# Early chunks of a fused retention, attention and spectral kernel in another order: V of chunk 0 behind the visit of chunk 1, the loads of chunk 1 ahead of V's weights, the decay table made by ScalarE, no second warm-up

## The chip, the cores and the metric

The kernel runs on one core of a Trainium2 chip. A core has TensorE (PE, matrix products), VectorE (DVE), ScalarE (ACT), GpSimd (POOL) and SyncE (SP, which issues nearly all transfers), each with its own list of instructions that it works off in order. The metric is the device time of one execution in microseconds (us). TensorE's clock has two levels, 1.2 and 2.4 GHz; the profile gives the level that was granted as 0.50 or 1.00.

## The reference

Three stages follow each other. All is float32, the batch is 8, the sequence 576, the width 512 (8 heads of 64).

```python
# 1: retention (8 heads)
scores = q @ k.T / 8
ret = scores * Dmat              # gamma[h] ** (i - j) for i >= j, else 0
x = ret @ v                      # heads side by side: [8, 576, 512]
# 2: four experts, two of them per token by x @ w_gate
for e in range(4):
    a = softmax(causal(x @ wq[e] @ (x @ wk[e]).T / 8))
    out += weight[..., e] * (a @ (x @ wv[e]) @ wo[e])
# 3: mixing
theta = out @ w_theta
y = w_tok_r @ (out * cos(theta)) + w_tok_i @ (out * sin(theta))
u = out + y
result = u + relu(u @ w_ch)
```

## The kernel before

Retention is computed in chunks of 128 tokens, five per batch (the last has 64), with a running state. For a chunk there are, all on PE with 64x64 tiles: the **scores** of its two halves (`ret_scores`, line 143), two **states** (`ret_state`, line 158, products of the chunk's k with its decayed v, called `vp`), and the **values** (`ret_values`, lines 173 and 180, which use the masked scores `sm`, `vp` and the states). A **visit** of chunk c here means the call of `ret_first` that computes the values of chunk c, interleaved product by product with the second state of c, and with the scores and the first state of chunk c+1. The result is scaled by a decay table `gt` (line 190, DVE) to `xt`, and split into a high and a low part `xh` (ACT, line 192) and `xl` (POOL, line 193), because the later products are run as three products of rounded parts.

`vp` is made by POOL in `scale()` (line 128) from the loaded `kv`. The table `gt` is loaded for 128 tokens and extended to the other chunks by `make_gt` (line 439). For stage 2, `proj_v` (line 273, "V of chunk c": 12 products of 128x260) and `proj_qk` (line 245) multiply `xh` and `xl` with the parts `WH`, `WL` of the expert weights; these parts are made from the loaded `wst` by ACT and DVE (lines 106 and 107), the columns of V first.

Batch 0 has no earlier work to hide behind. Its five chunks are written out by hand at the head of the program: the order of the calls is the order on PE, which is scheduled by hand there. On the other engines and on SP's queue an instruction stands where the call put it, or behind the one named by `issue_after`. Loads are issued by SP in the order written (`loads`, lines 117 and 120, is k and q, then k and v of a chunk); there are buffers for four chunks, so the load of the first chunk of batch 1 waits until the values of chunk 1 are done. `warm_up(n)` runs n small products on zeros.

The stretch that the change touches reads so before:

```python
ret_first(0, -1, (0, 0), [(0, 1)])      # scores and first state of chunk 0
ret_first(0, 0, None, [])               # second state and values of chunk 0
...                                     # split of V's weights, vp of chunk 1
warm_up(WARM2)
work(-1, "v0")                          # V of chunk 0
...
ret_first(0, -1, (0, 1), [(2, 3)])      # scores and first state of chunk 1
...
ret_first(0, 1, (0, 2), [(4, 5)])       # visit of chunk 1
...
ret_first(0, 2, (0, 3), [(6, 7)])       # visit of chunk 2
...
work(-1, "v1")                          # V of chunk 1
ret_first(0, 3, (0, 4), [(8,)])         # visit of chunk 3
work(-1, "v2 k00")
```

After that the batches run as a pipeline: attention of batch b beside the retention of batch b+1.

Of the kernel before, what the change touches and what calls it, by code (L numbers as in the profile page):

```python
# [15 lines left out]
AF = mybir.ActivationFunctionType  # L16
# [4 lines left out]
B, H, S, D = 8, 8, 576, 64  # L21
E, DM = 4, 512
C = 128
# [13 lines left out]
LDB = 4  # L37
# [8 lines left out]
         ("v0", "R3"), ("v1", "O"), ("v2 k00", "R4"), ("q00", "R5"), ("v3 k01 v4 g", "O")]  # L46
PTV = (0,)
WARM = 50
WARM2 = 10
WB = 8  # L50
JOBS = (58, 75)

# [11 lines left out]
def tile_kernel(ctx: ExitStack, tc: tile.TileContext, qk, kv, w1, wo, wot, wd, cst, out):  # L64
    nc = tc.nc
# [23 lines left out]
    gam = att.tile([128, NCH, 2, 4], F32, name="gam")  # L89
# [7 lines left out]
    gt = ret.tile([128, 4, S], F32, name="gt")  # L97
# [12 lines left out]
    MARK = {}  # L110
    QKT, KVT, XT, VP, SM, RAW = {}, {}, {}, {}, {}, []

    def loads(b, c):
        R = ROWS[c]
        o = c * 1024
        t = ret.tile([128, 8 * R], F32, name="kt", bufs=LDB, padded_shape=[128, 1024]).rearrange("p (h r) -> p h r", h=8)
        nc.sync.dma_start(t, qk[b, :, o:o + 8 * R].rearrange("p (h r) -> p h r", h=8))
        n = R // 64
        u = ret.tile([128, 2, 2, 256], F32, name="kv", bufs=LDB)
        nc.sync.dma_start(u[:, :n], kv[b, c, :, :n * 512].rearrange("r (j a d) -> r j a d", j=n, a=2))  # L120
        QKT[b, c], KVT[b, c] = t, u
        RAW.append((b, c))

    def scale():
        b, c = RAW.pop(0)
        n, u = ROWS[c] // 64, KVT[b, c]
        vp = ret.tile([128, 2, 4, D], F32, name="vp", bufs=VPB)
        MARK["pool"] = nc.gpsimd.tensor_mul(vp[:, :n], u[:, :n, 1, :].rearrange("p j (h d) -> p j h d", h=4),
                                            gam[:, c, :n, :, None].to_broadcast([128, n, 4, D]))
        VP[b, c] = vp  # L130

    def half(x):
# [2 lines left out]
    def ret_scores(b, ks):  # L135

        n = len(ks)
        ps = ps1.tile([128, n, 4, 64], F32, name="w", bufs=WB, padded_shape=[128, 2, 4, 64])
        for i, k in enumerate(ks):
            t, j = QKT[b, k // 2], k % 2  # L140
            for x in range(4):
                for s in range(2):
                    nc.tensor.matmul(ps[half(s), i, x, :], t[half(s), 4 + x, half(j)], t[half(s), x, half(j)],  # L143
                                     start=True, stop=True, skip_group_check=True)
                yield
        sm = ret.tile([128, n, 4, 64], F32, name="sm", bufs=4, padded_shape=[128, 2, 4, 64])
        MARK["sm"] = nc.vector.tensor_mul(sm, ps, tri[:, None, None, :].to_broadcast([128, n, 4, 64]))  # L147
        for i, k in enumerate(ks):
            SM[b, k] = sm[:, i]

    def ret_state(b, k):

        c, j = divmod(k, 2)
        u, vp = KVT[b, c], VP[b, c]
        pS = ps1.tile([128, 4, D], F32, name="w", bufs=WB, padded_shape=[128, 4, 128])
        for x in range(4):
            for s in range(2):
                nc.tensor.matmul(pS[half(s), x, :], u[half(s), j, 0, x * D:x * D + D], vp[half(s), j, x, :],  # L158
                                 start=x == 0, stop=x == 3, skip_group_check=True)
            yield  # L160
        o = SB[(k + 1) % 4]
        MARK["S"] = nc.vector.tensor_add(o, pS, SB[k % 4]) if k else nc.scalar.activation(o, pS, AF.Copy)

    def ret_values(b, c):

        R = ROWS[c]
        t, vp = QKT[b, c], VP[b, c]
        px = ps1.tile([128, 4, R], F32, name="w", bufs=WB, padded_shape=[128, 4, 128])
        for j in range(R // 64):
            sm = SM.pop((b, 2 * c + j))  # L170
            for x in range(4):
                for s in range(2):
                    nc.tensor.matmul(px[half(1 - s), x, half(j)], vp[half(s), j, x, :], sm[half(s), x, :],
                                     start=j == 0 and x == 0, stop=False, skip_group_check=True)
                yield
        for j in range(R // 64):
            k = 2 * c + j
            for x in range(4 if k else 0):
                for s in range(2):
                    nc.tensor.matmul(px[half(1 - s), x, half(j)], SB[k % 4][half(s), x, :], t[half(s), x, half(j)],  # L180
                                     start=False, stop=False, skip_group_check=True)
                yield
        for x in (QKT, KVT, VP):
            x.pop((b, c))
        cs = slice(c * C, c * C + R)
        if c == 0:
            XT[b] = (w1p.tile([128, 4, S], F32R, name="xh", bufs=1),
                     w1p.tile([128, 4, S], F32R, name="xl", bufs=1))
        xt = ret.tile([128, 4, R], F32, name="xt", bufs=2, padded_shape=[128, 4, 128])
        MARK["xt"] = nc.vector.tensor_mul(xt, px, gt[:, :, cs])  # L190
        xh, xl = XT[b]
        MARK["xh"] = nc.scalar.activation(xh[:, :, cs], xt, AF.Copy)  # L192
        MARK["xl"] = nc.gpsimd.tensor_sub(xl[:, :, cs], xt, xh[:, :, cs])  # L193
        nx = (b, c + LDB) if c + LDB < NCH else (b + 1, c + LDB - NCH)
        if nx[0] < B:
            loads(*nx)
# [19 lines left out]
    def ret_first(b, c, nx, scores):  # L216

        diag, off = [], []
        if c > 0:
            scale()  # L220
        if 0 <= c < NCH - 1:
            diag.append(ret_state(b, 2 * c + 1))
        diag += [ret_scores(nx[0], ks) for ks in scores]
        if nx and nx[1] < NCH - 1:
            diag.append(ret_state(nx[0], 2 * nx[1]))
        if c >= 0:
            off.append(ret_values(b, c))
        for _ in zip_longest(chain(*diag), chain(*off)):
            pass
# [74 lines left out]
    def work(b, names):  # L304
        for n in names.split():
            x = b + n.islower()
            if x < B:
                if n in "Gg":
                    gate(x)
                elif n[0] == "T":  # L310
                    token_tile(ps1, 0, len(X2))
                elif n[0] == "F":
                    fuse(int(n[1]))
                elif n[0] in "Vv":
                    proj_v(x, int(n[1]))
                else:
                    proj_qk(x, int(n[1]), int(n[0] in "Kk"), int(n[2]))
# [98 lines left out]
    def warm_up(n):  # L416
        pw = ps1.tile([128, 128], F32, name="w", bufs=WB, padded_shape=[128, 512])
        for _ in range(n):
            nc.tensor.matmul(pw, warm, warm, start=True, stop=True)
# [12 lines left out]
    gf = w1s.tile([128, 4, NCH], F32, name="gf")  # L432
# [3 lines left out]

    def make_gt(c):
        R = ROWS[c]
        nc.vector.tensor_mul(gt[:, :, c * C:c * C + R], gt[:, :, :R], gf[:, :, c, None].to_broadcast([128, 4, R]))

    wst = {}

    def load_w1(a, z):
        wst[a] = w1s.tile([128, 4, z - a], F32, name=f"wst{a}", bufs=1)
        nc.sync.dma_start(wst[a], w1.rearrange("(k p) n -> p k n", p=128)[:, :, a:z])

    def split_w1(a, k):
        t = wst[a]
        sl = slice(a, a + t.shape[2])
        split(WH[:, k, sl], WL[:, k, sl], t[:, k])  # L450

    load_w1(512, NW1)
    for c in range(1, LDB):
        loads(0, c)
    load_w1(0, 512)
    nc.sync.dma_start(tie, cst[:, o + 1088:o + 1088 + E * E].rearrange("p (a b) -> p a b", a=E))
# [75 lines left out]
    def fuse(p):  # L532
        acc = ps1.tile([128, DM], F32, name="w", bufs=WB)
        for kt, (th, wt) in enumerate(FW):
            mm3(acc, wt[:, 0, p, :], wt[:, 1, p, :], th[:, 0, :], th[:, 1, :], kt == 0, kt == 3)
        split(MH[:, p, :], ML[:, p, :], acc)

    ret_first(0, -1, (0, 0), [(0, 1)])
    ret_first(0, 0, None, [])
    for k in range(2):  # L540
        with tc.issue_after(MARK["xt"].ins), tc.issue_after(MARK["xh" if k else "S"].ins):
            split_w1(512, slice(2 * k, 2 * k + 2))
    with tc.issue_after(MARK["xl"].ins):
        scale()
    warm_up(WARM2)
    work(-1, "v0")
    with tc.issue_after(MARK["split"].ins):
        make_gt(1)
    ret_first(0, -1, (0, 1), [(2, 3)])
    scale()  # L550
    with tc.issue_after(MARK["pool"].ins):
        nc.gpsimd.dma_start(cm, cst[:, o:o + 1088])
    with tc.issue_after(MARK["sm"].ins):
        make_gt(2)
    ret_first(0, 1, (0, 2), [(4, 5)])
    for c in range(3, NCH):
        with tc.issue_after(MARK["xt"].ins):
            make_gt(c)
    ret_first(0, 2, (0, 3), [(6, 7)])
    for k in range(4):  # L560
# [92 lines left out]
    for t in range(nu + 1):  # L653
        b, k = divmod(t, 10)
        if b < B - 1:
            more, between, after = *SLOTS[k], ""
        else:
            b = B - 1
# [22 lines left out]
        if b < B - 1:  # L681
            if between[:1] == "R":
                c = int(between[1])
                x = b + 1
# [14 lines left out]
        i = int(t >= JOBS[0])  # L699
        x = t - JOBS[0] if i else t - 2  # L700
# [284 lines left out]
```

## Time and profile before

| | us |
|---|---|
| median of 3 runs | 880.44 |
| lowest and highest run | 877.99 and 881.26 |
| the profiled execution's own time | 879.58 |
| its span, first to last instruction | 877.8 |
| PE busy in the span | 859.2 (98%) |
| DVE, ACT, POOL busy | 622.0, 454.6, 218.7 |

The span is what the trace covers; 1.78 us of the execution's time lie around it. A busy share of 98% says that PE is the engine that sets the time, so what matters is where PE stands still or runs at the lower clock. "issue" in the profile is time in which an engine waited for nothing that the profile shows.

### The profile page before, as it was taken

Reading aid. Unit: us, or ns where it says so; the run is one execution under the profiler, and the core shown is the slowest. Engines: PE = TensorE matmul, PEld = TensorE weight load, DVE = VectorE, ACT = ScalarE, POOL = GpSimd, SP = SyncE. Lnnn points to the kernel's source line nnn. Section 1 sums busy time; section 2 is a strip of 40 time slices with the busy share of each in tenths; the row PEclk is TensorE's granted clock in tenths of the full one; section 3 lists DMA queues with packets and bytes.
Section 4 is the critical chain, followed back from the end, with each engine's and each line's share of the span. In section 5 each row is a group of like instructions: output and inputs, shape, how many; then the busy total and the mean of one; then the engine's idle time right before and its main releaser. Section 6 shows DMA issues by size and latency. Waiting matters only on the chain.

```text
span 877.8 us, 25574 instructions
## 1 busy us (share of the span) xinstructions
PE 859.2 (98%) x10072; PEld 795.2 (91%) x10072; DVE 622.0 (71%) x1729; ACT 454.6 (52%) x1258; POOL 218.7 (25%) x268
## 2 busy tenths in 40 slices
PE   6999999999999999999999999999999999999998
PEld 6989889888888989898789999999989999999998
DVE  4588787878788886876678777676377665766632
ACT  1366667666666766666576445353244533444320
POOL 3325253443525453341300012010210103001010
PEclk9899999999999999999999999999999999999999
DMA  9857677676867676548674442422525233241411
GB/s 317 246 155 239 171 221 199 194 224 187 255 169 222 202 211 179 160 108 238 185 265 170 83 111 47 120 37 61 141 57 139 62 96 93 34 124 25 100 34 54
DMA packets 140440, 130.30 MB, mean 148 GB/s; under 512 B 75808, under 2 KB 114976, under 8 KB 140320
## 3 DMA queue, kind: packets, MB, share of 16 engines
q1 hardware_dynamic: 140176, 128.39, 52.6%
q8 instruction: 79, 1.29, 0.6%
q0 software_dynamic: 144, 0.28, 0.2%
q14 instruction: 41, 0.34, 0.1%
HBM read 78.03 MB, written 32.00 MB: 125 GB/s over the span
## 4 chain that ended last, share of the span: by engine, by line
PE 88%; DMA 4%; DVE 3%; ACT 1%; issue 1%; POOL 1%; SPq 0%; ACTq 0%; DVEq 0%; POOLq 0%
PE acc L787 22%; PE w L245 11%; PE w L101 6%; PE w L102 6%; PE w L103 6%; PE w L335 6%; PE w L273 6%; PE w L401 5%; PE w L382 5%; PE w L787 3%; PE w L158 3%; PE w L143 3%; DMA kt<-qk 2%; DMA KK<-KN 1%; PE w L180 1%
## 5 line engine op out<-in xcount | busy, mean ns | idle before, releaser
L787 PE MATMUL acc<-TK,zh 128*128 128x288 f32 (+2 forms) x896 | 156.4, 296 | 0.5 <-ACT ob L405 0.5
L787 PEld LDWEIGHTS acc<-TK,zh 128*128 128x128 f32 x896 | 132.1, 189 | 1.2 <-issue 0.6
L343 ACT ACTIVATE P<-P,st 128x128 f32<-128x128 f32 (+4 forms) x160 | 95.4, 598 | 42.2 <-DVE st L338 41.9
L803 POOL TENSOR_TENSOR ul<-u,uh 128x576 fp32r<-128x576 f32 x16 | 24.2, 1531 | 309.6 <-ACT uh L802 309.6
L787 PE MATMUL acc<-TK,zl 128*128 128x288 f32 (+1 forms) x448 | 95.9, 295 | 0.0
L106 ACT ACTIVATE zh<-cs 128x512 fp32r<-128x512 f32 x64 | 40.3, 630 | 76.6 <-PE acc L787 61.4
L335 PE MATMUL w<-KK,U 128*64 128x288 f32 (+4 forms) x384 | 76.6, 327 | 1.5 <-DMA KK<-KN 1.4
L107 DVE TENSOR_TENSOR zl<-cs,zh 128x512 fp32r<-128x512 f32 x64 | 45.1, 705 | 43.2 <-ACT zh L106 42.5
L338 DVE CUSTOM_DVE_ANT_0 P<-w,cm 128x128 f32<-128x128 f32 (+4 forms) x160 | 71.1, 477 | 4.8 <-PE w L335 3.9
L787 PEld LDWEIGHTS acc<-TK,zl 128*128 128x128 f32 x448 | 72.4, 189 | 0.0
L626 ACT ACTIVATE cs<-cs,quarter 128x256 f32<-128x256 f32 x72 | 36.5, 507 | 55.4 <-DVE cs L624 55.2
L629 DVE SCALAR_TENSOR_TENSOR cs<-cs,x 128x512 f32<-128x512 f32 x72 | 50.7, 706 | 20.1 <-ACT cs L627 19.4
L382 PE MATMUL w<-ident,P 128*128 128x128 f32 (+2 forms) x480 | 60.1, 260 | 1.6 <-DVE sm L147 1.3
L335 PEld LDWEIGHTS w<-KK,U 128*128 128x128 f32 (+1 forms) x384 | 54.0, 171 | 8.0 <-DVE nwt L355 1.5
L193 POOL TENSOR_TENSOR xl<-xt,xh 128x512 fp32r<-128x512 f32 (+1 forms) x40 | 47.8, 1195 | 45.4 <-ACT xh L192 45.4
L479 POOL TENSOR_TENSOR r<-r,ex 128x192 f32<-128x192 f32 (+1 forms) x51 | 29.5, 578 | 116.2 <-ACT hl L480 42.0
L192 ACT ACTIVATE xh<-xt 128x512 fp32r<-128x512 f32 (+1 forms) x40 | 23.5, 589 | 66.9 <-DVE xt L190 66.8
L103 PE MATMUL w<-uh,CH 128*128 128x288 f32 x192 | 56.6, 295 | 0.0
L102 PE MATMUL w<-ul,CH 128*128 128x288 f32 x192 | 56.5, 294 | 0.0
L101 PE MATMUL w<-uh,CH 128*128 128x288 f32 x192 | 56.5, 294 | 0.0
L401 PE MATMUL w<-PT,V 128*64 128x192 f32 (+3 forms) x576 | 56.4, 325 | 0.0
L382 PEld LDWEIGHTS w<-ident,P 128*128 128x128 f32 (+2 forms) x480 | 47.1, 138 | 8.3 <-DVE sm L147 2.7
(153 smaller groups left out, 2340.4 us busy)
## 6 DMA issues: line engine op xcount, KB each, us to landing
KK<-KN SPq DMA_DIRECT2D x128, 144.0 KB
kt<-qk SPq DMA_DIRECT2D x32, 512.0 KB
kv<-kv SPq DMA_DIRECT2D x32, 512.0 KB
raw<-wd SPq DMA_DIRECT2D x43, 192.0 KB
xd<-xb SPq DMA_DIRECT2D x126, 64.0 KB
out<-u SPq DMA_DIRECT2D x28, 288.0 KB
u<-xd SPq DMA_DIRECT2D x28, 288.0 KB
td<-hl SPq DMA_DIRECT2D x27, 192.0 KB
```

The lines of the kernel that those rows point to most:

```text
L101: nc.tensor.matmul(ps, ah, bh, start=first, stop=False)
L102: nc.tensor.matmul(ps, ah, bl, start=False, stop=False)
L103: nc.tensor.matmul(ps, al, bh, start=False, stop=last)
L245: nc.tensor.matmul(ps, W[:, kt, w0:w0 + 128], x[:, kt, sl], start=x is xh and W is WH and kt == 0, stop=x is xl and kt == 3)
L273: nc.tensor.matmul(ps[:R], x[:, kt, cs], W[:, kt, w0:w0 + NV], start=x is xh and W is WH and kt == 0, stop=x is xl and kt == 3)
L335: nc.tensor.matmul(ps[s][:R], U[:, s, rs], KK[:, s, x, j0:j1], start=x == 0, stop=x == 1)
L338: MARK["dve"] = nc.vector.tensor_tensor_reduce(Ps[s][:R, j0:j1], ps[s][:R], cm[:R, o + j0:o + j1], 1.0, st[:R, 0, s:s + 1] if i else 3.0e3 ...
L343: MARK["act"] = nc.scalar.activation(Ps[s][:R, :n], Ps[s][:R, :n], AF.Exp, bias=st[:R, last, s:s + 1], scale=-1.0, accum_out=SUM[p][:R, m, ...
L382: nc.tensor.transpose(tp[:w, j, :], Ps[s][:R, j * C:j * C + w], ident[:R, :R])
L401: nc.tensor.matmul(po[s * 64:s * 64 + 64, c0:], V[:ROWS[j], j, 2 * p + s, :], v, start=j == 0, stop=j == last, skip_group_check=True)
L629: nc.vector.scalar_tensor_tensor(z, cs, -1.0, x2[:, None, ds].to_broadcast([128, 2, 256]), op0=OP.mult, op1=OP.mult)
L787: nc.tensor.matmul(acc[d][j], A[:, dc], TK[:, kt, W, t0:t1], start=q == 0 and n == 0, stop=q == 8 and n == 2)
```

## The change

V of chunk 0 moves on PE from behind the values of chunk 0 to behind the visit of chunk 1. SP loads chunk 1 before V's weights `wst` instead of after them. The second warm-up (10 products) goes. `make_gt` is done by ACT, four instructions per chunk, instead of one by DVE. The decayed `vp` of chunk 0 is made in halves, the first by DVE and the second by POOL. The split of V's weights stands later on ACT and DVE, behind the `xh` of chunk 0 and the last state addition that the visit of chunk 1 needs.

```diff
@@ scale
-        MARK["pool"] = nc.gpsimd.tensor_mul(vp[:, :n], u[:, :n, 1, :].rearrange("p j (h d) -> p j h d", h=4),
-                                            gam[:, c, :n, :, None].to_broadcast([128, n, 4, D]))
+        x, y = u[:, :n, 1, :].rearrange("p j (h d) -> p j h d", h=4), gam[:, c, :n, :, None].to_broadcast([128, n, 4, D])
+        i = 0
+        if (b, c) == (0, 0):
+            nc.vector.tensor_mul(vp[:, :1], x[:, :1], y[:, :1])
+            i = 1
+        MARK["pool"] = nc.gpsimd.tensor_mul(vp[:, i:n], x[:, i:], y[:, i:])
@@ ret_first
-        if c > 0:
+        if c >= 0:
             scale()
@@ make_gt
-        nc.vector.tensor_mul(gt[:, :, c * C:c * C + R], gt[:, :, :R], gf[:, :, c, None].to_broadcast([128, 4, R]))
+        for a in range(4):
+            nc.scalar.activation(gt[:, a, c * C:c * C + R], gt[:, a, :R], AF.Copy, scale=gf[:, a, c:c + 1])
@@ loads
+    loads(0, 1)
     load_w1(512, NW1)
-    for c in range(1, LDB):
+    for c in range(2, LDB):
         loads(0, c)
@@ the head of the program
     ret_first(0, -1, (0, 0), [(0, 1)])
+    make_gt(1)
     ret_first(0, 0, None, [])
+    ret_first(0, -1, (0, 1), [(2, 3)])
     for k in range(2):
-        with tc.issue_after(MARK["xt"].ins), tc.issue_after(MARK["xh" if k else "S"].ins):
+        with tc.issue_after(MARK["S"].ins), tc.issue_after(MARK["xh"].ins):
             split_w1(512, slice(2 * k, 2 * k + 2))
-    with tc.issue_after(MARK["xl"].ins):
-        scale()
-    warm_up(WARM2)
-    work(-1, "v0")
-    with tc.issue_after(MARK["split"].ins):
-        make_gt(1)
-    ret_first(0, -1, (0, 1), [(2, 3)])
-    scale()
+    with tc.issue_after(MARK["split"].ins), tc.issue_after(MARK["xh"].ins):
+        make_gt(2)
+    ret_first(0, 1, (0, 2), [(4, 5)])
     with tc.issue_after(MARK["pool"].ins):
         nc.gpsimd.dma_start(cm, cst[:, o:o + 1088])
-    with tc.issue_after(MARK["sm"].ins):
-        make_gt(2)
-    ret_first(0, 1, (0, 2), [(4, 5)])
+    work(-1, "v0")
     for c in range(3, NCH):
-        with tc.issue_after(MARK["xt"].ins):
+        with tc.issue_after(MARK["xt"].ins), tc.issue_after(MARK["xh"].ins):
             make_gt(c)
```

PE before, from the last values of chunk 0 on (`kt` holds k and q, `w` is a PSUM tile; a row is a product with its count):

```order
L180 MATMUL w<-kt,S_136 64x64 x8
...
L419 LDWEIGHTS warm
L419 MATMUL w<-warm 128x128
L273 MATMUL w<-WH,xh 128x260 x4
L273 MATMUL w<-WL,xh 128x260 x4
L273 MATMUL w<-WH,xl 128x260 x4
L143 MATMUL w<-kt 64x64 x16
L158 MATMUL w<-vp,kv 64x64 x10
L173 MATMUL w<-sm,vp 64x64 x2
```

PE of the change at the same place and at the end of the visit of chunk 1 (lines 183, 146, 161, 176 and 276 are the former 180, 143, 158, 173 and 273):

```order
L183 MATMUL w<-kt,S_136 64x64 x8
L146 MATMUL w<-kt 64x64 x16
L161 MATMUL w<-vp,kv 64x64 x10
L176 MATMUL w<-sm,vp 64x64 x2
...
L161 MATMUL w<-vp,kv 64x64 x2
L183 MATMUL w<-kt,S_138 64x64 x2
L276 MATMUL w<-WH,xh 128x260 x4
L276 MATMUL w<-WL,xh 128x260 x4
L276 MATMUL w<-WH,xl 128x260 x4
L161 MATMUL w<-vp,kv 64x64 x2
L176 MATMUL w<-sm,vp 64x64 x2
```

The warm-up products are gone, the scores of chunk 1 follow chunk 0 at once, and the 12 products of V stand between the visits of chunks 1 and 2. In a trace a 64x64 float32 product is two weight loads and two matmuls, one of V is one of each.

SP's queue of the change (the former order had `wst` ahead of the two loads above it):

```order
L433 DMA tri<-cst 128x64
L436 DMA gf<-cst 128x4x5
L437 DMA gt<-cst 128x4x128
L116 DMA kt<-qk 128x1024
L119 DMA kv<-kv 128x1024
L449 DMA wst_219<-w 128x4x260
L116 DMA kt<-qk 128x1024
L119 DMA kv<-kv 128x1024
```

The loads of chunk 1 moved up by one place, past 520 KB of weights.

ACT of the change, from its first state copy on:

```order
L165 ACTIVATE S_136<-w 128x256
L443 ACTIVATE gt<-gt,gf 128x128 x4
L195 ACTIVATE xh<-xt 128x4x128
L443 ACTIVATE gt<-gt,gf 128x128 x4
L105 ACTIVATE WH<-wst_219 128x2x260 x2
L195 ACTIVATE xh<-xt 128x4x128
L279 COPY V<-w 128x256
L280 ACTIVATE lg_126<-w 128x4
L443 ACTIVATE gt<-gt,gf 128x128 x4
L443 ACTIVATE gt<-gt,gf 128x64 x4
L195 ACTIVATE xh<-xt 128x4x128
```

The 16 `gt` rows are new on ACT, and the split of V's weights (`WH`) stands behind eight of them; before, its first half stood ahead of the `xh` of chunk 0.

## Rows read from the trace of the kernel before

**Rows 1.** The page: PE's busy time, and the queue that loads instructions (packets, MB).

```profile
PE 859.2 (98%) x10072; PEld 795.2 (91%) x10072; DVE 622.0 (71%) x1729; ACT 454.6 (52%) x1258; POOL 218.7 (25%) x268
...
q8 instruction: 79, 1.29, 0.6%
```

**Rows 2.** Stretches: length, busy us and counts by engine, granted clock, DMA share, GB/s.

```profile
15.00:20.00 5.00, 2.68 (x141) 2.46 (x137) 3.14 (x5) 0.00 (x0) 2.74 (x3) 1.00 1.04 384
...
30.00:35.00 5.00, 5.00 (x119) 4.77 (x117) 3.67 (x8) 1.26 (x4) 2.13 (x3) 1.00 0.87 326
```

**Rows 3.** The chain of waits, first 40 us: start, us, what.

```profile
14.12 1.10 PE w L143 x32
...
25.76 2.78 PE w L273 x12
...
30.57 1.63 PE w L273 x12
```

**Rows 4.** Stretches cut at PE's stops, for the counts of matmuls and weight loads.

```profile
0.00:8.14 8.14, 6.02 (x95) 5.78 (x96) 0.85 (x3) 1.28 (x1) 1.60 (x11) 1.00 0.78 217
0.00:15.16 15.16, 11.59 (x222) 10.56 (x224) 5.38 (x8) 3.91 (x7) 4.34 (x13) 1.00 0.90 304
0.00:17.90 17.90, 14.11 (x349) 12.86 (x350) 8.03 (x13) 3.91 (x7) 6.04 (x15) 1.00 0.92 318
20.70:23.95 3.25, 3.16 (x127) 2.96 (x126) 2.81 (x6) 0.63 (x1) 1.04 (x1) 0.61 0.92 217
25.05:31.20 6.15, 6.13 (x125) 5.81 (x126) 4.36 (x6) 3.04 (x7) 2.73 (x2) 0.74 0.76 217
```

**Rows 5.** Instruction queue in 11.5 to 12.7, 18.3 to 19.5, 22.2 to 23.7 us.

```profile
q8 instruction: 1, 0.02, 5.6%
...
q8 instruction: 1, 0.02, 5.8%
...
q8 instruction: 1, 0.02, 6.1%
```

**Rows 6.** PE's timeline: what runs first after its two stops.

```profile
20.74 0.27 PE L180 MATMUL w<-kt,S 64*64 64x64 f32 x2 [2.85 <-issue]
...
25.07 0.37 PE L180 MATMUL w<-kt,S 64*64 64x64 f32 x2 [1.17 <-issue]
```

**Rows 7.** POOL's timeline: vp of chunks 0 and 2, and of the half-size chunk 4.

```profile
6.64 1.04 POOL L128 TENSOR_TENSOR vp<-kv,gam 128x512 f32<-128x512 f32 x1 [5.55 <-DMA kv<-kv]
...
15.86 1.04 POOL L128 TENSOR_TENSOR vp<-kv,gam 128x512 f32<-128x512 f32 x1 [1.88 <-DMA kv<-kv]
...
24.19 0.61 POOL L128 TENSOR_TENSOR vp<-kv,gam 128x256 f32<-128x256 f32 x1
```

**Rows 8.** DVE's timeline: a state addition, a decay table, the split of Q's and K's weights.

```profile
9.01 0.42 DVE L162 TENSOR_TENSOR S<-w,S 128x256 f32<-128x256 f32 x1 [1.45 <-PE w L158]
...
13.01 1.53 DVE L439 TENSOR_TENSOR gt<-gt,gf 128x512 f32<-128x512 f32 x1
...
27.87 4.01 DVE L107 TENSOR_TENSOR WL<-wst,WH 128x512 fp32r<-128x512 f32 x4 [1.22 <-ACT WH L106]
```

**Rows 9.** ACT's groups by shape, first 60 us: count, busy us, mean ns.

```profile
L405 ACT COPY ob<-w 128x128 f32<-128x128 f32 x1 | 0.3, 261 | 0.0
```

**Rows 10.** Stretches around the fall and the rise of the clock.

```profile
18.00:21.00 3.00, 0.26 (x17) 0.26 (x20) 0.39 (x1) 0.00 (x0) 1.03 (x1) 1.00 1.09 350
...
21.50:25.00 3.50, 2.40 (x90) 2.21 (x82) 2.53 (x6) 0.63 (x1) 1.90 (x2) 0.50 0.91 272
25.00:28.20 3.20, 3.13 (x23) 3.01 (x24) 1.36 (x3) 1.51 (x3) 0.81 (x1) 0.50 0.63 172
```

**Rows 11.** SP's queue: the issue of batch 1's first chunk.

```profile
21.22 0.33 SPq L117 DMA_DIRECT2D kt<-qk  x1
```

**Rows 12.** All waits of one kind, first 36 us: total us, times, longest us.

```profile
PE w L273 <- ACT xh L192: 0.8, 1, 0.8
...
PE w L273 <- DVE WL L107: 0.6, 1, 0.6
```

More of the change, by code (lines that the diff above doesn't have):

```diff
@@ L48 @@
 WARM = 50
-WARM2 = 10
 WB = 8
```

## The prediction

> **What bounds the kernel now.** The page comes first: PE is busy for 98% of the span [rows 1], and from 30 us on the stretches show it full [rows 2]. Whatever moves the start of that unbroken run moves the end. Both programs have the same order on PE from V of chunk 1 on, which starts at 25.76 [rows 3], so the prediction is the start of V of chunk 1 after the change.
>
> Before that point the waits show four stops on PE: 0.8 for `xh` and 0.6 for `WL` inside V of chunk 0 [rows 12], and 2.85 and 1.17 with no releaser [rows 6]. The reader should ask what the last two are, since they are the larger. The page has a queue that carries instructions, 79 packets of 1.29 MB together [rows 1]: 16.3 KB each, and 2 x 10072 matmuls and weight loads over 79 are 255 a packet. The stretches count 349 + 350 = 699 instructions up to the first stop and 127 + 126 = 253 between the first and the second [rows 4]. One packet lies in the window that ends at 19.5 and one in that which ends at 23.7 [rows 5]; PE goes on at 20.74 and 25.07 [rows 6], about 1.3 later each time. So I read both stops as code that has not arrived: PE gets its program in blocks of some 254, and the block after a boundary is asked for when the boundary before it is crossed. Counted back from 699, the boundaries before lie near 446 and 192, which PE reached at 15.16 and 8.14 [rows 4]. Crossing to code ready took 20.74 - 15.16 = 5.6 and 25.07 - 20.74 = 4.3. For the first block the packet ends by 12.7 [rows 5], so 12.7 + 1.3 - 8.14 = 5.9 at most; PE came later than that, at 15.16, because V of chunk 0 had held it up.
>
> The Trainium skill (Runtime: NRT & Kernel Launch, section Instruction fetch mechanics) says that engines fetch their program in 16 KiB blocks of 256 instructions, the next while the current one runs; the trace agrees with 253 between the stops. It also says that crossing a boundary is mostly hidden, and by that the 4.0 us of stops would belong to the order of the work and could go with it, which is the second rival below. The trace speaks against it here, as the stops lie 253 apart and end behind the packets.
>
> **The change part by part.** *`vp` of chunk 0 in halves.* POOL's whole took 1.04 from 6.64; a half costs POOL 0.61 [rows 7], and on DVE no row shows it; the nearest, an addition of 128x256, took 0.42 [rows 8], and at worst it costs POOL's 0.61. The first state needs only DVE's half, so chunk 0 starts 0.4 to 0.6 earlier; I take 0.5. The boundary near 192 is crossed at 7.6, and the masked scores follow on DVE 0.4 later than before, which the earlier states cover.
>
> *Loads of chunk 1 ahead of V's weights, V later.* Scores of chunk 1 (1.10 [rows 3]) now follow chunk 0 directly, where before V stood with its 1.4 of waits. By then V's weights, `xh` and `xl` have had several us: V itself waits for nothing and costs the 1.63 that 12 products took at full clock [rows 3].
>
> *Where the code boundaries now fall.* Up to the end of chunk 0 there are 100 warm-up instructions and 56 products of four, 324. Scores (64) and first state (32) of chunk 1 make 420, so the boundary near 446 is crossed at the start of the visit of chunk 1. The visit (state 32, scores 64, state 32, values 128) ends at 676 and V (24) at 700: the next boundary is V's last product. The visit of chunk 2 (256) ends at 956, so the third lies four instructions ahead of V of chunk 1. With the second warm-up it was 24 ahead, 25.76 - 25.07 = 0.69 of work; now about 0.15.
>
> *The chain of blocks.* First block: 7.6 + 5.9 = 13.5 as the upper end; I take 13.4. PE gets to the boundary near 446 before that: up to chunk 1's `kv` the loads now hold 2.42 MB, of which 8.14 x 217 = 1.77 MB are in by 8.14 and 15.16 x 304 - 1.77 = 2.84 MB more by 15.16 [rows 4], so `kv` lands near 9.8, `vp` is there near 11 (1.04 on POOL), and 26 more instructions lead to the boundary by 11.5. The wait for code thus moves here, some 1.9. Second block: 13.4 + 5.6 = 19.0. PE does not come before that either: the state of chunk 2 needs `vp` at 15.86 + 1.04 = 16.9 [rows 7], as the bytes ahead of its `kv` are the same ones in another order; about 0.5 later the visit ends, 17.4, and V takes 1.63, 19.0. V fills what was the 2.85 stop. Third block: 19.0 + 4.3 = 23.3 or 19.0 + 5.6 = 24.6. The 4.3 was measured while the queues moved 217 GB/s, the 5.6 while they moved some 384 [rows 2, 4]. Batch 1's first loads, issued at 21.22 before [rows 11], wait for the values of chunk 1 and now go out near 17.5, so the third packet meets full queues: I take 5.3, nearer the second, 24.3. PE has done the visit of chunk 2 by about 21 and stands for over 3 us: the stop grows, though it ends earlier.
>
> *Edits at nothing.* Sixteen pieces of `gt` on ACT cost at most 0.26 each, 4.2 in all (a piece of this size took 0.26 [rows 9]; below that only the 64-wide ones). Four sit ahead of `xh` of chunk 0, under DVE's `xt`; four ahead of V's split, with V due 4 us later; eight in 15 to 20 us, where ACT did nothing [rows 2]. If that cover were gone, each group of four would cost 1.0. DVE gives up pieces of up to 1.53 [rows 8] that nobody waited for. The split of K's and Q's weights, 4.01 on DVE [rows 8], hangs on the values of chunk 2 and moves with them; it ended ahead of its use by 0.6 or so and may take back that much.
>
> *The clock.* With 0.26 busy of 3.00 the clock fell, and stayed at 0.50 until 28.2 [rows 10]; V of chunk 1 took 2.78 for 1.63 [rows 3]. The new stop ahead of V of chunk 1 is as long, so I keep V of chunk 1 at the lower level and count no gain.
>
> **The sum.** V of chunk 1 starts at 24.3 + 0.15 = 24.45 against 25.76: 1.3 less. The ends: 23.45 with a third block of 4.3 (2.3 less), 24.75 with 5.6 (1.0 less), and 0.5 less if the halves gain nothing. On the profiled execution's own 879.58 that is 878.3; the execution lies 0.86 below the median of the runs, and the same step from 880.44 gives 879.1. Later boundaries lie 18 instructions further on in the work, worth some tenths either way, with the split's 0.6 the reason to widen the range.
>
> **The rivals.** *Nothing comes through:* the third block's wait ends where it did, or the K and Q split holds PE, 880.4. For it: three blocks in a row of 5.9, 5.6, 5.6 from 8.14 end at 25.2. Against: an earlier first crossing.
>
> *The stops go:* code is not what PE waits for. Then 0.8 + 0.6 [rows 12] and 2.85 + 1.17 [rows 6] are free, the clock holds and V of chunk 1 saves 1.15: 6.6, giving 873.8. A part of it, with blocks of 4.3 throughout (first ready 11.9, second with V at 19.0, third 23.3) and the clock held, is 2.3 + 1.15 = 3.5, 877.0.
>
> *Slower, the clock falls early:* with no second warm-up and PE waiting for `vp`, code and `kv` between 10.5 and 17, the clock falls ahead of V of chunk 0. V then takes 2.78, ends at 20.2 and crosses its boundary 1.2 later: third block 25.5, V of chunk 1 at 25.65, no gain left. After the long stop the lower level then also covers the visit of chunk 3 and V of chunk 2, 1.15 for V of chunk 2 alone and as much for the visit: 2.3 slower, 882.7. It decides if the granted clock is 0.50 while V of chunk 0 runs. For it: three waits of 1 to 2 us lie in a row there, where before V and the scores stood. Against: in this trace the clock fell only behind a stretch that was all but empty [rows 10], and none of the three is that. The Trainium skill (TensorE: Matmul & The Clock Gate, section Why this matters for your kernels) warns of idle gaps between bursts of matmuls as what drops the clock, and by that this rival is what the change invites; the trace shows the fall behind the 2.85 stop.
>
> **How the numbers follow.** Forecast 0.52; nothing 0.18; the stops go, in whole 0.04, in part 0.10; the early fall 0.16. The runs of before spread over 3.3 us, so a median can lie 1 off. The range 876.4 to 882.4 takes in the partial gain and nearly the early fall. A change of 0.5% is 4.4 us, about what a measurement of this kernel can tell from none: below 876.0 only the full rival lies, with a little noise 0.07; above 884.8 only the early fall with more stages at the lower level, 0.04; the rest, 0.89, is within.
>
> **What would show it.** Right: a stop without a releaser of 1 to 2.5 us that ends near 13.4, none or a tenth ahead of the visit of chunk 2, one of 3 or more that ends near 24.3 directly ahead of V of chunk 1, with some 253 instructions between stops; no wait inside V of chunk 0. Wrong: the third stop missing, or ending after 25, or a granted clock of 0.50 before 20 us.

## The result, and the profile after

The changed kernel took 887.91 us (median of 4 runs, 886.23 to 889.99), the kernel before 879.22 beside it (4 runs, 876.63 to 881.26): a ratio of 1.01, interval 1.0069 to 1.013. It is 8.7 us slower. Forecast were 879.1 with a range up to 882.4. The profiled execution took 889.34 us, its span is 887.6.

The page of the changed kernel, PE's line. Against [rows 1] PE is busy for 3.2 us more, although it has ten products less; the granted clock, 0.996 before as a mean, is 0.992.

```profile
PE 862.4 (97%) x10062; PEld 798.7 (90%) x10062; DVE 618.6 (70%) x1726; ACT 460.3 (52%) x1274; POOL 218.3 (25%) x268
```

The chain of waits of the changed kernel, first 40 us (start, us, what), answers to [rows 3]: V of chunk 0, the stop ahead of V of chunk 1, then V of chunks 1 and 2.

```profile
18.17 3.13 PE w L276 x12
...
23.32 3.44 issue
...
27.09 2.15 PE w L276 x12
...
32.24 1.63 PE w L276 x12
```

V of chunk 1 starts at 27.09, forecast was 24.45, and before it was 25.76 [rows 3]. Where it went wrong is seen in the stretches of the changed kernel, cut first at the three boundaries between code blocks, then at the changes of the clock (length, busy us and counts of PE, PEld, DVE, ACT, POOL, granted clock, DMA share, GB/s).

```profile
0.00:13.03 13.03, 9.75 (x223) 9.10 (x223) 3.36 (x8) 4.75 (x11) 3.61 (x13) 1.00 0.85 284
13.03:20.77 7.74, 6.28 (x128) 5.65 (x127) 3.51 (x7) 1.79 (x3) 3.62 (x5) 0.58 1.05 388
20.77:26.76 5.99, 2.56 (x128) 2.24 (x128) 1.45 (x3) 2.56 (x10) 1.08 (x2) 0.97 0.68 228
...
14.60:21.40 6.80, 6.35 (x116) 5.67 (x120) 2.42 (x5) 0.69 (x2) 4.01 (x4) 0.52 1.06 369
...
28.30:31.60 3.30, 3.30 (x85) 3.07 (x85) 2.50 (x2) 2.66 (x7) 2.73 (x2) 0.53 0.83 295
```

The counts are as predicted, 446 instructions up to the first boundary and some 255 in each block. The times are not: the second block took 7.74 from crossing to crossing where 5.6 was forecast, the third 5.99 where 5.3 was. The granted clock was 0.52 from 14.6 to 21.4, which is the third rival's condition, and again 0.53 behind the long stop.

PE's timeline around the first boundary (start, us, what, idle before and what ended it): PE stood for `vp` and `kt` of the next chunks, and hardly for code.

```profile
11.94 0.62 PE L161 MATMUL w<-vp,kv 64*64 64x64 f32 x14 [1.27 <-POOL vp L132]
...
13.03 0.27 PE L176 MATMUL w<-sm,vp 64*64 64x64 f32 x2 [0.18 <-issue]
...
14.73 0.37 PE L146 MATMUL w<-kt 64*64 64x64 f32 x2 [1.13 <-DMA kt<-qk]
```

In all, the changed kernel is 1.3 us late at V of chunk 1 and, with the lower clock in 28.3 to 31.6, 1.7 us late at V of chunk 2. The greater part comes later, in stretches where both kernels do the same work in the same order. PE's timeline of the changed kernel in the batches:

```profile
122.36 0.21 PE L146 MATMUL w<-kt 64*64 64x64 f32 x1 [1.70 <-issue]
...
175.88 0.27 PE L183 MATMUL w<-kt,S 64*64 64x64 f32 x2 [1.31 <-issue]
...
227.99 0.21 PE L183 MATMUL w<-kt,S 64*64 64x64 f32 x1 [1.48 <-issue]
...
280.68 0.27 PE L161 MATMUL w<-vp,kv 64*64 64x64 f32 x2 [1.64 <-DVE sm L150]
...
384.56 0.27 PE L161 MATMUL w<-vp,kv 64*64 64x64 f32 x1 [1.94 <-issue]
```

One stop in each of five batches, 8.1 us in all. (The fourth names DVE: that `sm` ended at 280.17, half a microsecond before PE went on, while a packet of code had ended at 279.32, 1.36 before, as at the others. So it is counted with them, but a part of it may be a wait for `sm`.) In the kernel before the batches had 0.9 of such stops. Behind the first of them the granted clock also fell for a while, which it does not there in the kernel before. The first stretch below shows the clock; the other two, from stop to stop, tell why the stops come back:

```profile
124.00:127.20 3.20, 3.20 (x18) 2.86 (x19) 0.92 (x5) 2.06 (x7) 1.93 (x2) 0.54 0.93 276
...
122.36:175.88 53.52, 52.21 (x883) 47.13 (x883) 41.25 (x142) 33.40 (x109) 22.19 (x32) 0.97 0.68 194
175.88:227.99 52.11, 50.63 (x881) 45.73 (x882) 41.90 (x142) 33.38 (x109) 22.86 (x32) 1.00 0.70 203
```

1766 and 1763 instructions lie from stop to stop, seven blocks of 252. The same product comes again, one batch later, after 1760 (counted in both traces at the products of lines 385 and 382). A batch is thus very nearly seven blocks long, so a boundary that meets a bad place in one batch comes within a few instructions of it in the next ones too.

What happens at such a place is seen one boundary earlier. In the changed kernel PE crosses it at 115.94 (252 instructions ahead of the stop) and the next block's load starts at 119.84. SP's queue of the changed kernel, then the instruction queue in 119.8 to 120.8, then two stretches:

```profile
114.29 0.56 SPq L116 DMA_DIRECT2D kt<-qk  x1
114.94 0.87 SPq L119 DMA_DIRECT2D kv<-kv  x2
117.54 3.01 SPq L360 DMA_DIRECT2D gd<-nwt  x4
...
q8 instruction: 1, 0.02, 5.7%
...
117.90:119.80 1.90, 1.90 (x62) 1.67 (x65) 1.90 (x10) 0.76 (x2) 0.34 (x2) 1.00 0.94 384
119.80:121.80 2.00, 0.86 (x57) 0.73 (x48) 1.93 (x4) 2.00 (x12) 1.37 (x1) 1.00 0.23 35
```

The same in the kernel before, where PE crosses that boundary at 113.08, 18 instructions earlier in the work; the last line is the instruction queue in 112.8 to 114.2:

```profile
111.55 0.56 SPq L117 DMA_DIRECT2D kt<-qk  x1
112.20 0.87 SPq L120 DMA_DIRECT2D kv<-kv  x2
...
q8 instruction: 1, 0.02, 4.7%
```

There the block had been ready some 1.6 us before PE came to it (its load ended at 110.15, and the stops end some 1.3 to 1.6 after a load; 1.35 is taken here), and the load of the next one started at 112.91, before PE's crossing. In the changed kernel the same margin is 0.5 us (114.05 and 115.94). At the like boundary of the next four batches the kernel before came 1.5, 1.2, 1.3 and 0.7 us after its code was ready, and the load started 1.2, 0.8, 1.1 and 2.9 us behind the crossing; at its five stops the changed kernel came 0.0 to 0.5 us after, and the load started 3.3 to 4.0 behind. One reading is that code is here asked for behind the loads of `kt` and `kv` and starts when the queues fall from 384 to 35 GB/s; PE, which ran through the block before in 3.1 us (112.82 to 115.94), has saved up little and stands. The experiments below put this reading to the test and do not bear it out in every batch.

### The profile page after: what moved, and what is told of

It reads as the page before. It is cut to its first block, busy times and chain, and to the rows that moved or that the text cites. A ratio compares the mean times of both kernels' runs of the same rounds, so it can differ in the third digit from the quotient of the medians.

```text
span 887.6 us, 25571 instructions
## 1 busy us (share of the span) xinstructions
PE 862.4 (97%) x10062; PEld 798.7 (90%) x10062; DVE 618.6 (70%) x1726; ACT 460.3 (52%) x1274; POOL 218.3 (25%) x268
## 4 chain that ended last, share of the span: by engine, by line
PE 91%; DMA 3%; issue 2%; DVE 2%; ACT 1%; POOL 1%; SPq 0%; ACTq 0%; DVEq 0%; POOLq 0%
PE acc L787 22%; PE w L248 11%; PE w L338 7%; PE w L276 7%; PE w L100 6%; PE w L101 6%; PE w L102 6%; PE w L404 6%; PE w L385 5%; PE w L787 3%; PE w L161 3%; PE w L146 3%; DMA kv<-kv 2%; DMA KK<-KN 1%; PE w L183 1%
```

## The experiments

Theory after the result: the PE instructions that the change leaves out move every later boundary by 18 instructions of work; that costs some 7 us in the batches, and the new order itself about 1. Rival: the late start and the lower clock early on are what the batches carry along. A second question was what a late block waits for.

**e1_pairs_back**: the 18 instructions back, at a place where PE has time. (The change takes out ten products, 20 recorded instructions, but nine bring the boundaries back: the block that starts at 324.92 in e1 and that which starts at 323.25 in the kernel before begin with the same product, 8867 recorded instructions ahead of the end in both.)

```diff
     ret_first(0, 0, None, [])
+    warm_up(9)
     ret_first(0, -1, (0, 1), [(2, 3)])
```

> The changed kernel with nine warm-up products put back behind the values of chunk 0, 18 instructions, so that from there on every instruction stands at the same place in its code block as before. If the batches' stops come from where the block boundaries fall, the five stops of 1.3 to 1.9 us between 120 and 385 us go, about 7 us in all, and it takes 880 to 882. If they come from the new order of transfers or engines, they stay and it takes 887 to 888. The clock ahead of V of chunk 0 may hold with the products back, which would give another 1 us.

880.74 us (10 runs, 878.72 to 884.75), ratio 1.001 [0.9987, 1.0033]. The stops in the batches are gone but for one of 0.75; V of chunk 1 starts at 27.05, as late as in the changed kernel, V of chunk 2 at 30.70 against 32.17 (PE's timelines).

**e2_before_18_fewer**: the kernel before, in its own order, with 18 instructions less.

```diff
-WARM2 = 10
+WARM2 = 1
```

> The kernel before with one product in its second warm-up instead of ten, 18 instructions fewer, and nothing else. If the block boundaries make the batches' stops, it gets stops of 1.3 to 1.9 us at the same five places as the changed kernel and takes 885 to 887. If the order does, it stays at 879 to 880. If the missing warm-up brings the clock down early, the granted clock is 0.50 between 14 and 21 us and the start costs 1 to 2 us.

886.04 us (5 runs), ratio 1.0075 [1.0039, 1.0112], which is 6.6 us. PE's timeline of this run, four of its stops:

```profile
71.15 0.27 PE L143 MATMUL w<-kt 64*64 64x64 f32 x1 [1.47 <-issue]
...
123.42 0.21 PE L143 MATMUL w<-kt 64*64 64x64 f32 x1 [1.09 <-issue]
...
175.24 0.27 PE L180 MATMUL w<-kt,S 64*64 64x64 f32 x2 [1.31 <-issue]
...
227.35 0.21 PE L180 MATMUL w<-kt,S 64*64 64x64 f32 x1 [1.49 <-issue]
```

With nothing moved, nine dummy products less make the kernel 6.6 us slower. It has five stops of 1.1 to 1.5 in the batches, the fifth at 279.88, again 1766 instructions or so apart; four are in batches in which the changed kernel has one, while that at 71.15 is new and that near 384 missing. One of 2.41 ahead of 38.05 comes on top. And with one product left of the second warm-up but V of chunk 0 in its old place the granted clock stays up until behind the long stop, which ends at 20.77:

```profile
4.30:21.40 17.10, 10.96 (x347) 9.68 (x348) 8.89 (x13) 2.63 (x6) 6.52 (x6) 0.99 1.05 370
```

So the missing warm-up alone does not bring the early fall of the clock; it takes the new order. How early it comes there differs from run to run: 14.3 in the changed kernel, 16.8 in e1, 18.8 in e5.

**e3_before_96_more**: the kernel before with 48 products of 32x32 behind the first warm-up.

```diff
     warm_up(WARM)
+    pad(48)
```

> The kernel before with 48 products of 32x32 on zeros behind the first warm-up, 96 instructions more. From the times between instructions 256 apart in the trace of before, boundaries moved by 96 leave the longest time for each block, so if the blocks set the stops it loses the stops of 0.3 to 0.6 it had in the batches, about 1.2 us, and pays up to 1 us at the head: 877 to 880. If blocks do not matter it takes 879.5 to 880.5 plus the cost at the head, up to 1 us.

878.09 us (10 runs), ratio 0.9987 [0.9962, 1.0011]; no stop named "issue" behind 30 us. The time lies within both forecasts, so it does not tell them apart.

**e5_pairs_at_head**: the changed kernel with the 18 instructions at the very start.

```diff
-WARM = 50
+WARM = 59
```

> The changed kernel with 59 instead of 50 products in the first warm-up: the same shift by 18 instructions as with nine products behind chunk 0, but no work where PE waits for chunk 1. Blocks: the batches' stops go, 880 to 882. If it is the second warm-up as such, and its clock, that counts, the batches' stops stay here, 887. The early fall of the clock ahead of V of chunk 0 should stay, granted clock 0.50 from about 14.6 us.

880.58 us (10 runs), ratio 1.0008 [0.9989, 1.0028]. The total is as expected; four stops of 0.8 to 1.5 remained in the profiled execution, one of them a wait for `kt`, and the clock fell at 18.8, not at 14.6 as was expected.

**e4_after_114_more**: the changed kernel with 57 small products at the head, which puts the boundaries of the batches where e3 has them.

```diff
     warm_up(WARM)
+    pad(57)
```

> The changed kernel with 57 more small products of 32x32 behind the first warm-up: 114 instructions more, so from the batches on the boundaries between code blocks lie where they lie in e3_before_96_more. Theory (the place of the boundaries against the loads of data costs the time, the new order itself is worth about nothing): no stop over 1 us without a releaser in the batches, 877 to 880 us, level with the kernel before. Rival (the new order costs, through the clock that falls at 14.5 us and the long stop ahead of V of chunk 1): the early stretch stays some 2 us late and the batches do not give it back, 882 or more.

878.35 us (median of 10 runs, one of them at 3530.54), ratio 0.9986 [0.9963, 1.001]; no stop over 0.7 in the batches. V of chunk 1 starts at 25.61, no later than before.

**e6_pairs_late**: the 18 instructions behind the early stretch, so that only the later boundaries move back.

```diff
+    warm_up(9)
     w1s.release()
     work(-1, "v1")
```

> The changed kernel with 9 warm-up products (18 instructions) between the visit of chunk 2 and V of chunk 1, behind the third boundary: everything up to 26.8 us is that of the changed kernel, with its stops and its clock, and every boundary from the fourth on stands in the work where it stood in the kernel before. Theory (places of the later boundaries): V of chunk 1 at about 27.7 us, the stops of 1.3 to 1.9 us near 122, 175, 227, 280 and 384 us go, and what is left is the early delay: 881 to 883. Rival (the late and slow early stretch is the cause, the batches only carry it on): the stops in the batches stay, 887 to 889.

880.47 us (10 runs), ratio 1.0005 [0.9984, 1.0026]. The third boundary is that of the changed kernel, and V of chunk 1 comes 0.3 later, behind the nine products. The five stops are gone; one other has come:

```profile
26.50 0.33 PE L183 MATMUL w<-kt,S 64*64 64x64 f32 x2 [3.32 <-issue]
...
27.43 2.49 PE w L276 x12
...
325.89 0.27 PE L146 MATMUL w<-kt 64*64 64x64 f32 x2 [1.82 <-issue]
```

This settles theory against rival. The early stretch, with its stop and its clock, is unchanged, and 887.91 becomes 880.47: 7.4 us were the places of the later boundaries, the fall of the clock behind the first stop included. Nor is it the 0.3 us by which the nine products hold PE up: in e1 V of chunk 1 starts when it does in the changed kernel, and the stops go as well. How late the same product starts against the kernel before, read off the two traces in us:

```
time before     40    80   120   160   200   240   280   320   360   400   440   840
changed        1.7   2.7   6.1   5.9   6.7   7.0   8.9   8.9   8.3  10.4   9.5   9.8
e6             1.9   2.5   2.6   2.5   2.0   1.3   1.4   1.4   2.6   2.7   0.5   0.6
e2             2.6   4.4   5.8   5.5   6.0   6.4   8.1   8.1   7.5   7.5   6.4   6.4
```

The early 1.9 of e6 is mostly given back: between 400 and 440 us the kernel before waits 1.38 for `KK` from 426.6 on, a wait that a later kernel does not have in full.

**e7_late_loads** and **e9_later_loads**: what does the second block wait for? Both are e1 with the loads of chunk 3, K's and Q's weights and chunk 4 held back, behind the state addition of chunk 1 (e7) or the split of V's weights (e9).

```diff
-    for c in range(2, LDB):
-        loads(0, c)
-    load_w1(0, 512)
+    loads(0, 2)
...
+    d = loads(0, 3)
+    tc.add_manual_dep(d.ins, MARK["S"].ins.name, ...)   # e9: MARK["split"]
+    load_w1(0, 512)
+    loads(0, 4)
```

> e1_pairs_back with the loads of chunk 3, of the weights of K and Q, and of chunk 4 issued behind the first state addition of chunk 1 (about 13 us) instead of at the head of the program; PE's program is the same. Theory (a code block waits behind the transfers that are already queued when it is asked for): asked for at 12.9, the second block starts to load near 15.5 instead of 18.5, is ready near 18 instead of 21, and the stop of 1.94 us ahead of it goes below 0.5; V of chunk 1 comes 1 to 3 us earlier, 877.5 to 880. Rival (the load does not depend on the data queued ahead of it): it starts at 18.3 to 18.5 again, 880.7 or more, since chunk 3 comes later.

> As e7_late_loads, but the loads of chunk 3, of the weights of K and Q and of chunk 4 are issued behind the split of V's weights (about 15 us), so that they are not yet queued when PE asks for the second block at about 13.4 us; PE's program is that of e1_pairs_back. Theory (a code block waits behind the transfers queued ahead of it): the second block starts to load before 16.5 instead of 18.4, is ready before 19 instead of 20.6 to 21, and the stop of 2 to 2.6 us ahead of V of chunk 0 goes below 1. Rival (the load of code has its time from something else, such as the total traffic): it starts at 18.3 to 18.5 again. In the total, 878 to 881 by either, as chunk 3 and the third block come later in turn.

e7: 880.87 us, ratio 1.0012 [0.9988, 1.0036]; its second block was asked for at 13.53 and started to load at 18.35. The first held loads went out at 12.89 and 13.26, ahead of the boundary, so this run did not test the question. Its instructions on PE are those of e1, yet two stops named "issue" are back in its batches (1.57 ahead of 172.23, 1.27 ahead of 224.16): the place of a boundary alone does not settle whether its code is late. e9: 881.24 us, ratio 1.002 [1.0, 1.004]. There they went out at 14.84. Its stretches, and the instruction queue in 14.2 to 15.7:

```profile
13.00:14.00 1.00, 0.48 (x29) 0.34 (x21) 0.49 (x1) 1.00 (x2) 0.00 (x0) 1.00 0.82 288
14.00:15.00 1.00, 0.76 (x49) 0.79 (x53) 1.00 (x3) 0.00 (x0) 0.00 (x0) 1.00 0.15 45
15.00:16.00 1.00, 0.41 (x28) 0.27 (x19) 0.72 (x2) 0.00 (x0) 0.56 (x1) 1.00 0.38 56
...
q8 instruction: 1, 0.02, 4.9%
```

With the boundary crossed at 12.80, the second block started at 15.25, in queues that had been nearly empty since 14.5, and was ready at 17.77, 3.2 us earlier than in e1, which has the same program on PE. The theory held for this block. Nothing was won: the data of chunk 3 came later in turn, PE waited 3.36 for its `vp` up to 24.16, and the third and fifth loads of code stood behind the held loads (4.9 and 5.5 us from crossing to load; 3.06 of stop up to 39.26).

**e11_more_and_later_loads**: e4 with the loads of e9, as a candidate.

> e4_after_114_more with the later loads of e9_later_loads; a candidate for a version that beats both kernels. Theory: the second block starts to load before 15.8 instead of 16.3 us, the batches stay without stops over 1 us, 876 to 879. Rival: as e4_after_114_more or slower, 878 to 881, since chunk 3 comes later than it is wanted.

877.68 us (10 runs), ratio 0.9983 [0.9965, 1.0002]. Its stretches and PE's timeline:

```profile
13.00:14.00 1.00, 1.00 (x38) 1.00 (x38) 0.07 (x1) 1.00 (x3) 0.94 (x1) 1.00 0.90 332
14.00:15.00 1.00, 0.79 (x36) 0.65 (x36) 1.00 (x3) 1.00 (x4) 0.33 (x1) 1.00 0.33 91
...
16.96 0.27 PE L148 MATMUL w<-kt 64*64 64x64 f32 x1 [0.89 <-issue]
```

The split that the loads hang on came later here, so the queues, full until 13.6, were nearly empty from 14.5 to 17; the load started at 14.31, 1.46 after the crossing, the shortest of the five second blocks below.

The second block in five kernels, from the list of packets and PE's instructions, in us:

```
                  crossed   load starts   next crossing
before              15.16         18.35           20.74
changed             13.03         18.34           20.77
e1                  12.88         18.49           20.96
e9                  12.80         15.25           17.77
e11                 12.85         14.31           16.95
```

**e8_batch_loads_later**, **e10_half_loads** and **e12_loads_behind_gd**: the same question in the batches, on the changed kernel with PE's program unchanged. e8 makes the loads wait for the next state addition, e10 loads half the data (POOL sets the rest of the tiles to zero, which is work that the changed kernel does not have), e12 issues the loads that two of five visits set free one step later, behind `gd` where it stands between.

```diff
-            loads(*nx)
+            LATE.append(nx)                 # e8, e12: issued later
-        nc.sync.dma_start(t, ...)           # e10: 4 of 8 heads, 64 of 128 tokens
+        nc.sync.dma_start(t[:, :w], ...)
```

> The changed kernel, PE's program the same, but from batch 1 on the loads of k, q and kv wait in SP's queue until the first state addition of the next chunk, about 1.5 us later than now. Theory (the stops of the batches come from code that is asked for 1.0 to 1.7 us behind an issue of loads): the boundary that is crossed at 115.9 us, and its like in the later batches, now comes ahead of the loads; the code starts to load within 1 us instead of 3.3 to 3.9, the stops of 1.3 to 1.9 us shrink below 0.6, 881 to 884. Rival (the stops hang on what stands in those blocks of the program, not on the loads of data): they stay, 887 to 889.

> The changed kernel with only half of k, q and kv loaded from batch 1 on (half of the heads of k and q, the first 64 tokens of kv); the rest of the tiles is set to zero by POOL, so the values from batch 1 on are not the reference's. PE's program is word for word that of the changed kernel. Theory (the code of the batches waits behind the loads of data): the loads of code in the batches start within 2 us of the crossing instead of 3.3 to 3.9, no stop over 0.8 us without a releaser, 879 to 883. Rival (the stops hang on what stands in the blocks, which is unchanged): the stops of 1.3 to 1.9 us near 121, 175, 227, 280 and 384 us stay, 887 or more.

> The changed kernel with PE's program word for word the same; from batch 1 on the loads of k, q and kv that were issued 1 to 1.7 us ahead of the critical boundary (115.9 us and its like in later batches) are issued behind the four small transfers of gd, some 3 us later. Theory (code waits until the transfers in flight have drained, and the loads are what fills them): at those boundaries the code starts to load within 2 us of the crossing, the stops of 1.3 to 1.9 us near 121, 175, 227, 280 and 384 us go, 881 to 884. Rival (the code comes after gd whatever is in flight, as in three places of e10_half_loads, where it came 1.5 us after the transfers had drained): it still starts 3.3 to 4 us after the crossing, the stops stay, 886 to 889.

e8: 886.33 us, ratio 1.0069 [1.0046, 1.0092], again with five stops of 1.2 to 1.7 (up to 70.15, 122.98, 225.24, 277.68 and 381.26). `kt` was issued 1.65 us ahead of the boundary again (114.97 against 116.62): it stands behind another transfer in SP's queue that is itself late, and the new wait ended sooner. The edit did not bring the loads behind the boundary, so it does not test the question.

e10: 885.73 us (4 runs), ratio 1.0073 [1.0046, 1.0101]: a miss, between the two forecasts. Of the five stops the first is gone (its block now starts to load 1.4 us after the crossing), but four of 1.0 to 1.8 stay near 172, 225, 278 and 382. The first of them, in stretches:

```profile
165.65:166.90 1.25, 1.25 (x32) 1.18 (x24) 1.18 (x7) 0.47 (x3) 0.02 (x1) 1.00 0.00 0
166.90:168.20 1.30, 1.30 (x13) 1.16 (x12) 1.26 (x3) 0.20 (x1) 1.30 (x3) 1.00 0.55 151
168.20:169.60 1.40, 1.40 (x58) 1.21 (x60) 1.40 (x8) 0.32 (x1) 1.32 (x3) 1.00 0.01 1
169.60:171.00 1.40, 0.91 (x62) 0.77 (x54) 1.37 (x6) 1.40 (x7) 1.03 (x2) 1.00 0.07 14
```

PE crossed at 165.65, the load started at 169.62, and in between the queues were all but empty twice. Waiting behind data does not explain this one.

e12: 918.34 us, ratio 1.046 [1.0425, 1.0495], far off, for a reason of its own: `kt` now comes too late.

```profile
PE w L152 <- DMA kt<-qk: 22.6, 9, 3.7
```

At the boundaries in question the code did start to load 0.5 to 1.0 after the crossing in four of the five batches (3.3 to 4.0 in the changed kernel), but there PE came with 1.7 to 2.5 us of margin, as it had waited elsewhere; in the one batch without margin it took 3.0. So this does not settle it either.

## Why the prediction was wrong

**What bounds the kernel**: right in that PE's stops set the time and that the early ones are code; the counts put all three boundaries where the change has them. "Whatever moves the start of that unbroken run moves the end" took for granted that the run stays unbroken; with the stops in the batches it did not.

**"Later boundaries lie 18 instructions further on in the work, worth some tenths either way"**: this is the step that failed. They were worth 7.4 us (changed against e6), and 6.6 in the old order (e2). The result lies 8.8 above the forecast; the other 1.4 comes from the early blocks. I had the means to see that the step comes again: the same blocks run on through the batches, and a batch is very nearly seven blocks. By themselves 18 instructions are only some 0.2 us of 64x64 products (257 took 3.1 from 112.82 to 115.94); what they take away at the boundary read above is the margin, from 1.6 us to 0.5, and why so little work takes so much margin is not shown.

**First block, 13.4**: the code was ready at 13.03, near the forecast, but the stop of 1.9 us ahead of it was only 0.18. PE itself came 1.3 later than forecast, at 12.85 instead of 11.5, as it had stood 1.27 for `vp` of chunk 1 up to 11.94, where 11 was forecast.

**Second block, 19.0**: wrong, 20.77. I added 5.6 from crossing to ready. The crossing doesn't set it: the load starts near 18.35 whether the boundary is crossed at 15.16 or at 13.03, and e9, against e1, shows that the data queued ahead of it hold it up. The wait was sized in [rows 4] at one point and moved along; what should have been kept is the time at which the queues are free.

**Third block, 24.3**: wrong, 26.76, in part because it follows the second, and 5.99 for 5.3 by itself. That PE would stand over 3 us ahead of V of chunk 1 was right (3.44), its end was not, so that V of chunk 1 came 1.3 later instead of 1.3 earlier. The signs of being wrong that the prediction names were both there: a third stop that ends after 25, and a granted clock of 0.50 before 20 us.

**Edits at nothing**: in the early stretch no wait named `gt` or the split in the changed kernel. The halves of `vp` did let chunk 0 start earlier, the first boundary being crossed at 7.35 for 8.14.

**The clock, and the third rival**: its condition came true, the granted clock was 0.52 while V of chunk 0 ran (3.13, forecast for that case 2.78). Its first price was nothing: V ended at 21.3, and the code of its own last product was not there before 20.77. Its second, the lower clock behind the long stop, cost 1.5 at V of chunk 2 (32.17 against 30.70 in e1, where the clock was up again from 27.0 on), against 2.3 forecast for both; e6, which has it too, ends level with before. The Trainium skill (TensorE: Matmul & The Clock Gate, section Why this matters for your kernels) warns of idle gaps between bursts of matmuls; the trace agrees in that the clock fell at 14.3, in the second of two stops of 1.27 and 1.13 us; in e5 the two were 0.53 and 0.83, and the clock held until 18.8.

**The other rivals**: "nothing comes through" gives the time of e1, e5 and e6, that is of the change with its boundaries put back. "The stops go" did not happen in any kernel.

**What is open**: in the early stretch the second block of code waits for the transfers queued ahead of it (e9 against e1). In the batches the code behind four of the five stops of the changed kernel starts to load just as the queues drain, the fifth some 2 us after; in e10 four stay late at half the data, three of them with queues that had been empty for 1.5 us. What those wait for no run here shows, so it is shown that the places of the boundaries cost the time, and not by what a block at a bad place is held up. The Trainium skill (Runtime: NRT & Kernel Launch, section Instruction fetch mechanics) calls the crossing of a block mostly hidden; here it cost 8.1 us in the batches. The Trainium skill (DMA: Bandwidth & Descriptors, section Queues, rings and completion order) has each engine take turns between the queues packet by packet; by that a block of code that is in its queue from the crossing on would not stand 5.3 us behind data. At 13.03 it did, if it was in its queue by then, which the trace does not show.

No version beats both kernels clearly: e3, e4 and e11 lie 0.1 to 0.2% below the kernel before, within what the measurement can tell, and 1.1% below the changed one.

## What to carry to other kernels

Adding or removing a few instructions on a busy engine shifts every block of its code behind them; before believing that an edit at the head costs or gains by itself, put the count of instructions back with dummy work and time that too. Where stops named "issue" lie a fixed number of instructions apart, ask in which places of the loop the boundaries fall, and whether the loop is nearly a whole number of blocks long, because then one bad place can be paid in every turn. A wait that ends when a queue drains is to be kept as a time of that queue, not as a length counted from its request.

## What the runs showed of the hardware that was not expected

Nine dummy products more or less, 18 of some 20100 PE instructions, changed the time by 6.6 and by 7.4 us in two kernels. Where PE stood for code, the shortest way from crossing a boundary to ready code was 4.1 us, with queues that ran empty 1.6 us after the crossing (e11, 12.85 to 16.95), while PE ran through a block of 64x64 products in 3.1 (112.82 to 115.94). With a load that takes that long such a block is hidden only by a margin saved up before it, 1.6 us in the kernel before and 0.5 in the changed one at the boundary that was read.
